# An FNet, adaLN and SwiGLU block: the sequence DFT folded once more, with only every 32nd line corrected

## The chip, the cores and the metric

The kernel runs on one core of one Trainium2 chip. The metric is the device time of one execution in microseconds (us). Each kernel is executed several times; the median and the lowest and highest time are given. A profile of one further execution shows each engine: TensorE (PE, matrix products), VectorE (DVE), ScalarE (ACT), GpSimd (POOL) and SyncE (SP), and the 16 DMA engines. ScalarE, SyncE and GpSimd start the transfers.

## The reference, cut to what matters

S = 2048 rows, D = 512, F = 1792, one batch, all in f32.

```python
def _A_ref(x, dft_seq_re, dft_seq_im, dft_hid_re, dft_hid_im):
    a = jnp.einsum("bsd,ed->bse", x, dft_hid_re)
    b = jnp.einsum("bsd,ed->bse", x, dft_hid_im)
    return jnp.einsum("ts,bse->bte", dft_seq_re, a) - jnp.einsum("ts,bse->bte", dft_seq_im, b)

def _B_ref(x, w1, w3, w2):
    gate = jnp.einsum("bsd,df->bsf", x, w1)
    up = jnp.einsum("bsd,df->bsf", x, w3)
    return jnp.einsum("bsf,fd->bsd", _silu(gate) * up, w2)

mod = (_silu(c) @ w_mod).reshape(c.shape[0], 6, 1, -1)
sa, ca, ga, sb, cb, gb = (mod[:, 0], ..., mod[:, 5])
h = _layernorm(x, axis=-1) * (1 + ca) + sa
x = x + ga * _A_ref(h, ...)          # real part of a DFT over rows and columns
h = _layernorm(x, axis=-1) * (1 + cb) + sb
x = x + gb * _B_ref(h, ...)          # SwiGLU
```

`dft_seq_re` and `dft_seq_im` are 2048x2048 inputs, cos and sin of -2 pi t s / S; a kernel may use their symmetry only if it also verifies it on the chip.

## The kernel before, in words

`folded` is the main path. Every f32 product that must be exact is split into a high and a low part (type fp32r) and done in three passes, high by high, high by low, low by high (`PASSES`). `copy` and `minus` make the parts: ScalarE copies the high part (L87), VectorE subtracts for the low part (L90). Names that end in `h` and `l` are such parts. `minus`, `plus` and `times` (L90, L93, L96) are the VectorE helpers; nearly all its work carries their lines.

**Stage 1, hidden DFT.** Eight blocks k pair 128 rows with the 128 rows mirrored to them. For each: `load_x`, `norm_stats` (L456), scale, `turn_rows` (PE transposes, L492), `modulate_rows`, sums and differences of mirrored rows (`mirror_sums`, tile `hs`), their parts `hh`, `hl`, then `hid_product` (L566, 24 matmuls of 128x256), `hid_difference` (L583) and `hid_mirror` (L605, L614: the DFT of the mirrored rows alone, which serves the correction). The results are `us`, `ul` (sums' high and low part) and `uh`. The order is set by `arrange`, a list planner: each task has a rank, the tasks it needs, and an engine with an assumed time. Before the stage's data are there, `keep_warm` issues matmuls on zeros.

**Stage 2, sequence DFT.** 16 steps of two `seq_unit` each (real and imaginary, m = 0, 1), each 24 matmuls of 128x512 (L757), summed in all 8 PSUM banks. The symmetry halves the rows that must be multiplied: high parts `bh` of the matrix lines are used, plus the tiles `l` and `d`, the differences of the lines from what exact symmetry would give, so any deviation is corrected in full. `load_seq` reads the whole matrix for that (tiles `re`, `im`): 64 direct loads on SP and 64 gathers of mirrored lines on POOL (`load_mirror`, L170). `prepare_seq` makes `bh`, `l`, `d` on VectorE; ScalarE sums their squares (`square`, L188). `residual` (L813) adds the gated result to x.

**Stage 3, SwiGLU.** The second norm, `ln2`, is feature-major (L825 and on): sums over partitions through VectorE's 32x32 transposes. It goes in pieces on the queue `background`, which `advance` and `drain` empty beside the matmuls. Up-products of the first two column groups g = 0, 1 for the first half of the tokens (pair 0) are plain (`up_block`); the others are items (g, pair) and use `factor`, seven products in place of eight (Strassen's form), units a1 to a7 (w1) and b1 to b7 (w3). Down-products are plain (`down_unit`), except in the list `SEVEN` (pair 1, g = 0 to 4), where `seven_unit` does them by seven products. Each y of 512 KB is added to `sums` in HBM by an accumulating DMA on POOL; the last go from SBUF to the output. Near the end `judge` reduces the squares to a flag `bad`; where it is set, `general`, a kernel without the symmetry, runs.

VectorE and ScalarE work in program order, so an instruction that waits holds all that are behind it on that engine. SP and POOL issue their transfers in order too.

Of the kernel before, what the change touches and what calls it, by code (L numbers as in the profile page):

```python
# [15 lines left out]
P = 128  # L16
# [14 lines left out]
AHEAD = 3  # L31
# [11 lines left out]
def folded(nc, pools, c, cp, wmr, wmc, x, xt, ctr, cti, wdr, wdi, w1, w3, w2, out):  # L43

    consts, small, big, psum, dram, tc = pools


# [15 lines left out]
    def bank(i):  # L70
        count[0] += 1
        return psum.tile([P, N], F32, name=f"bank{i}_{count[0]}", tag=f"bank{i}")
# [36 lines left out]

    background = deque()  # L110
    credit = [0.0, 0.0]
# [5 lines left out]
    def advance(dve, act=9.0, queue=background):  # L117

        for n, us in enumerate((dve, act)):
            credit[n] = min(credit[n] + us, max(us, 1.0))  # L120
        while queue and len(free) >= queue[0][0] + kept():
            _, *cost, fn = queue[0]
            if any(us > 0 and credit[n] <= 0 for n, us in enumerate(cost)):
                return
            queue.popleft()
            if fn is None:
                return
            for n, us in enumerate(cost):
                credit[n] -= us
            fn()  # L130

    def drain(ready, queue=background):
# [6 lines left out]
    loads = deque()  # L139

    def kept():
        return 2 if loads else 0


    def where(k):
        return k % (NK // 2), 1 - k // (NK // 2)

    mirror = consts.tile([P, NT, 2, NK // 2], I32, name="mirror")  # L150
    flips = consts.tile([P, 2, NT, 2, NK // 2], I32, name="flips")
    nc.gpsimd.iota(
        mirror, [[S, NT], [2, 2], [-2 * P, NK // 2]], base=S - 1, channel_multiplier=-2
    )
    nc.gpsimd.iota(
        flips[:, 0], [[0, NT], [0, 2], [0, NK // 2]], base=0, channel_multiplier=1
    )
    nc.gpsimd.memset(flips[:, 1], 0)
    nc.gpsimd.memset(flips[0:2, 1, :, 1], 1 - 2 * P)
    nc.gpsimd.memset(flips[0:1, 1, :, 1], -1)  # L160
    nc.gpsimd.memset(flips[0:1, 1, :, 1, 0:1], -1 - S // 2)
    nc.vector.tensor_scalar(flips[:, 0], flips[:, 0], 1, None, op0=OP.bitwise_and)
    for n in range(2):
        plus(mirror, mirror, flips[:, n])

    def load_mirror(dst, src, k, t=None):
        i, par = where(k)
        rows = src.rearrange("i p q n -> (i p q) n" if t is None else "t i p q n -> (t i p q) n")
        at = mirror[:, t or 0, 1 - par, i : i + 1]
        nc.gpsimd.indirect_dma_start(  # L170
            dst, None, rows, bass.IndirectOffsetOnAxis(ap=at, axis=0)
        )

    KINDS = ("re", "im", "wr", "wi")
    chk = consts.tile([P, 2, 4, 32], F32, name="chk")
    nc.gpsimd.memset(chk, 0.0)
    used = {}

    def square(kind, m, src, junk):
# [12 lines left out]
        return n  # L194

# [6 lines left out]
    def load_x(k, other=nc.sync):  # L202
        if k >= NK // 2:
            nc.gpsimd.tensor_copy(held, wd[0][0:1, 1, 0:1].bitcast(F32))


        i, par = where(k)
        xz[k] = take(F32, "x")
        nc.sync.dma_start(xz[k][:, 0, :], x[i][par::2])
        if par:  # L210
            other.dma_start(xz[k][:, 1, :], x[NK - 1 - i][1::2])
        else:
            load_mirror(xz[k][:, 1, :], x, k)
# [7 lines left out]

# [10 lines left out]

    nc.sync.dma_start(cc, cp)
    load_x(0, nc.scalar)
# [9 lines left out]
    for k in range(2, 4):  # L244
        load_x(k)

# [30 lines left out]

    def keep_warm(count, width=N):

# [6 lines left out]
    nc.scalar.activation(sc, cc, AF.Silu)  # L286
    nc.scalar.activation(held, eps[0:1, 0:1], AF.Sqrt)
    mod1 = consts.tile([P, 2, ND], F32, name="mod1")
    ga = consts.tile([P, ND], F32, name="ga")
    ga2 = consts.tile([P, ND], F32, name="ga2")  # L290
# [5 lines left out]

# [21 lines left out]

# [25 lines left out]
    sc_row = []  # L344

    def mod_row():
        sc_row.append(take(F32, "scr"))
        nc.sync.dma_start(sc_row[0][:, 0, :], c.broadcast_to([P, D]))
        nc.scalar.activation(sc_row[0][:, 0, :], sc_row[0][:, 0, :], AF.Silu)

    def mod_columns(v, dst):
        w = {}

        def fetch(i):
            w[i] = take(F32, "wmc")
            nc.sync.dma_start(w[i], wmc[v, i])

        def scale(i):
            times(w[i], w[i], sc_row[0][:, 0, :].unsqueeze(1).to_broadcast([P, 2, N]))

        def total(i):
            r1 = small.tile([P, 32], F32, name=f"r1_{v}_{i}", tag="r1")
            nc.vector.tensor_reduce(
                out=r1,
                in_=flat(w[i]).rearrange("p (a b) -> p a b", b=32),
                axis=AX.X,
                op=OP.add,
            )
            nc.vector.tensor_reduce(
                out=dst[:, 2 * i : 2 * i + 2],  # L370
                in_=r1.rearrange("p (a b) -> p a b", b=16),
                axis=AX.X,
                op=OP.add,
            )
            give(w[i])

        def end():
            if dst is cb1:
                nc.vector.tensor_scalar(cb1, cb1, 1.0, None, op0=OP.add)
            if dst is ga:  # L380
                nc.vector.tensor_scalar(ga2, ga, -2.0, None, op0=OP.mult)
            if dst is gb:
                give(sc_row[0])
            done.add(("mod", v))

        for i in range(2):
            step(background, 1, lambda i=i: fetch(i))
        background.extend([PAUSE] * 2)
        for i in range(2):
            step(background, 0, lambda i=i: scale(i), 1.2)  # L390
            step(background, 0, lambda i=i: total(i), 1.3)
        step(background, 0, end, 0.1)


# [10 lines left out]

# [28 lines left out]

# [10 lines left out]

# [18 lines left out]

# [14 lines left out]

    turned, hm, hs, h1 = {}, {}, {}, {}  # L480
    hh, hl = {}, {}

    def sides(t):

# [2161 lines left out]
```

## Time and profile before

| | |
|---|---|
| median of 3 runs | 691.25 us (690.86 to 692.67) |
| span of the profiled execution | 688.6 us |
| TensorE / VectorE busy | 672.4 us (98%) / 586.2 us (85%) |
| ScalarE / GpSimd busy | 452.3 us (66%) / 133.6 us (19%) |
| stage 2 on the chain of waits | 86.19 to 260.5 us |
| moved by DMA | 116.8 MB |

The times in the profile count from the start of its span; the 2.65 us between the span and the median are start and end of the program outside it. A row of the groups reads: line, engine, operation, output and input by the program's names, shapes, count, then busy us, mean ns of one, and idle time of the engine just before, with what ended it. The windows give busy us and instruction counts of each engine for a stretch of time, then the granted TensorE clock, the mean busy share of the DMA engines and GB/s. Matmul durations in the groups (about 390 ns) overlap; their pace is read from the chain.

### The profile page before, as it was taken

The page shows a single profiled execution, that of the slowest core. Times are in us where ns is not written, and L with a number is a line of the kernel's source. Part 1 is how long each engine was busy: PE and PEld are TensorE (multiplying, and loading weights), DVE is VectorE, ACT ScalarE, POOL GpSimd, SP SyncE. Part 2 cuts the span into 40 slices and gives each one's busy share as a digit, 9 for nine tenths or more (in the row PEclk, how much of TensorE's full clock was granted, in tenths as well). Part 3 has the DMA queues.
Part 4 walks back from the last instruction along what each step waited for, and adds up shares of the span by engine and source line. Part 5 has one row for each costly group of instructions (what it writes and reads, how often), then busy time and mean ns, then how long its engine had stood idle before and what let it go on. Part 6 is the DMA issues. An engine that isn't in the chain of part 4 may idle for free.

```text
span 688.6 us, 9030 instructions
## 1 busy us (share of the span) xinstructions
PE 672.4 (98%) x3120; PEld 557.3 (81%) x3120; DVE 586.2 (85%) x944; ACT 452.3 (66%) x753; POOL 133.6 (19%) x156
## 2 busy tenths in 40 slices
PE   7899999999999999999999999999999999999995
PEld 5798888888888888888788888887887888888784
DVE  5999779997999977989997989787998979888464
ACT  6998965455443665663577767867687887877520
POOL 1320273543435000100101101011011112121100
PEclk9999999999999999999999999999999999999999
DMA  8730299797688431263757666466958998999803
GB/s 265 225 123 1 62 363 352 256 304 239 195 285 289 153 148 31 50 135 122 132 135 135 149 153 123 93 116 134 283 89 186 173 203 168 177 218 172 191 31 127
DMA packets 40837, 116.80 MB, mean 170 GB/s; under 512 B 5200, under 2 KB 5456, under 8 KB 40784
## 3 DMA queue, kind: packets, MB, share of 16 engines
q0 software_dynamic: 14512, 50.86, 36.8%
q1 hardware_dynamic: 25840, 63.98, 28.1%
q10 hardware_dynamic: 432, 1.31, 0.6%
q8 instruction: 26, 0.43, 0.3%
q14 instruction: 27, 0.22, 0.1%
HBM read 76.81 MB, written 41.42 MB: 172 GB/s over the span
## 4 chain that ended last, share of the span: by engine, by line
PE 84%; DVE 9%; ACT 3%; DMA 2%; issue 1%; SPq 1%; DVEq 0%; ACTq 0%
PE bank L100 54%; PE bank L757 26%; PE bank L566 2%; PE bank L605 1%; DMA w<-in_wdr 1%; DMA w<-in_wdi 1%; SPq L231 1%; DVE xr L813 1%; PE bank L583 1%; DMA x<-in_x 1%; DVE v L96 1%; DVE hl L90 0%; DVE ul L90 0%; DVE x L93 0%; ACT hm L508 0%
## 5 line engine op out<-in xcount | busy, mean ns | idle before, releaser
L100 PE MATMUL bank<-hf,w2h 128*128 128x512 f32 (+1 forms) x352 | 108.3, 389 | 0.0
L87 ACT ACTIVATE hf<-v 128x512 fp32r<-128x512 f32 x71 | 44.4, 631 | 66.9 <-DVE v L96 56.4
L342 ACT ACTIVATE y<-bank,gb 128x512 f32<-128x512 f32 x118 | 76.6, 683 | 3.9 <-PE bank L100 3.6
L100 PEld LDWEIGHTS bank<-hf,w2h 128*128 128x128 f32 x352 | 65.6, 188 | 15.3 <-ACT y L342 1.4
L1168 POOL DMA_DIRECT2D sum<-y x28 | 24.0, 857 | 240.7 <-ACT y L342 124.5
L100 PE MATMUL bank<-hf,w2l 128*128 128x512 f32 (+1 forms) x176 | 68.1, 387 | 0.0
L90 DVE TENSOR_TENSOR hf<-v,hf 128x512 fp32r<-128x512 f32 x71 | 48.7, 686 | 10.4 <-ACT hf L87 10.3
L1360 POOL DMA_DIRECT2D sum<-y x35 | 29.8, 852 | 128.3 <-ACT y L342 113.7
L87 ACT ACTIVATE x<-bank 128x512 f32<-128x512 f32 x72 | 41.9, 592 | 13.1 <-PE bank L100 12.3
L170 POOL DMA_INDIRECT re<-in_ctr,mirror x32 | 37.0, 1157 | 66.5 <-ACT im L188 40.1
L757 PE MATMUL bank<-bh,us 128*128 128x512 f32 x128 | 49.9, 390 | 0.0
L757 PE MATMUL bank<-bh,ul 128*128 128x512 f32 x128 | 49.8, 389 | 0.0
L757 PE MATMUL bank<-d,us 128*128 128x512 f32 x128 | 49.8, 389 | 0.0
L757 PE MATMUL bank<-d,uh 128*128 128x512 f32 x128 | 49.8, 389 | 0.0
L757 PE MATMUL bank<-l,us 128*128 128x512 f32 x128 | 49.8, 389 | 0.0
L757 PE MATMUL bank<-l,uh 128*128 128x512 f32 x128 | 49.8, 389 | 0.0
L170 POOL DMA_INDIRECT im<-in_cti,mirror x32 | 33.3, 1042 | 31.6 <-PE bank L757 10.0
L100 PEld LDWEIGHTS bank<-hf,w2l 128*128 128x128 f32 x176 | 33.1, 188 | 6.7
L93 DVE TENSOR_TENSOR v<-bank,x 128x512 f32<-128x512 f32 x36 | 24.7, 686 | 15.8 <-PE bank L100 14.9
L1252 ACT ACTIVATE v<-v 128x512 f32<-128x512 f32 x36 | 22.7, 629 | 22.9 <-DVE v L93 22.6
L93 DVE TENSOR_TENSOR x<-bank,x 128x512 f32<-128x512 f32 x36 | 24.7, 685 | 14.8 <-PE bank L100 11.9
L188 ACT ACTIVATE im<-l 128x512 f32<-128x512 f32 x16 | 10.1, 632 | 32.3 <-DVE d L93 15.4
(263 smaller groups left out, 1922.0 us busy)
## 6 DMA issues: line engine op xcount, KB each, us to landing
sum<-y POOLq DMA_DIRECT2D x63, 512.0 KB, 5.6
w<-in_w SPq DMA_DIRECT2D x42, 512.0 KB, 4.8
re<-in_ctr SPq DMA_DIRECT2D x32, 256.0 KB, 5.2
im<-in_cti SPq DMA_DIRECT2D x32, 256.0 KB, 5.7
wmc<-in_wmc SPq DMA_DIRECT2D x8, 512.0 KB, 6.9
sum<-xr SPq DMA_DIRECT2D x8, 512.0 KB, 5.4
x<-in_x SPq DMA_DIRECT2D x11, 256.0 KB, 4.6
xr<-in_xt SPq DMA_DIRECT2D x8, 256.0 KB, 7.6
```

The source lines that it names most:

```text
L87: nc.scalar.activation(dst, src, AF.Copy, scale=scale)
L90: nc.vector.tensor_tensor(out=dst, in0=a, in1=b, op=OP.subtract)
L93: nc.vector.tensor_tensor(out=dst, in0=a, in1=b, op=OP.add)
L100: nc.tensor.matmul(acc, lhs[a], rhs[b], start=first and n == 0, stop=last and n == len(PASSES) - 1, skip_group_check=more,)
L170: nc.gpsimd.indirect_dma_start(dst, None, rows, bass.IndirectOffsetOnAxis(ap=at, axis=0))
L188: nc.scalar.activation(to, src.bitcast(F32), AF.Square, accum_out=chk[:, kind, KINDS.index(m), n : n + 1],)
L342: nc.scalar.activation(dst, src, AF.Identity, scale=by)
L566: nc.tensor.matmul(halves(hb[k])[:, m, :], sides((hh, hl)[a][k])[:, dt, m, :], wu[dt][:, b, m, :], start=False, stop=dt % 2 == 1 and n == ...
L757: nc.tensor.matmul(acc[what, e], lhs, rhs, start=begin and i == 0, stop=(end or (turn and what == "x")) and i == len(terms) - 1, skip_grou ...
L1168: nc.gpsimd.dma_start(sums[t, d // 2], y, accum_op=OP.add)
L1252: behind(k != 0 or q == 0, lambda: nc.scalar.activation(v, src, AF.Silu))
L1360: nc.gpsimd.dma_start(sums[t, which], y, accum_op=OP.add)
```

## The change

Parts named here are new unless a line of before is given.

1. *Sequence DFT, folded once more.* `hid_mirror`, `uh`, `prepare_seq` and `seq_unit` go. The output rows split in even and odd (o) and in mirrored halves; `seq_piece` multiplies only 512 of the 2048 output rows, as four blocks b of 128, by `mh`, `ml` (parts of the matrix, loaded directly by `load_m`). The two banks of a block, m = 0 and 1, are read after the odd part and after all (`read_odd`, `read_all`), and sums and differences of the two (`read_other`, `join`) give the four groups of rows, which `add_rows` adds to x.
2. *Correction.* Only every 32nd line and column is corrected. `stage_lines` copies these columns in HBM to `lines` (16 transfers on SP) and `load_lines` reads them; `line_columns`, `turn_lines`, `line_rows`, `line_products`, `row_products`, `line_pairs`, `line_shares` form small products whose result enters the banks in `seq_lines`. Coefficients per partition (`signs`, `whole`, some 65 VectorE instructions on one column) are made at the very start.
3. *Differences counted.* All other entries are compared for equality: `check_steps` loads the matrix in stage 3 (tiles `cx`, `cz` direct, `cy`, `cv` by gathers) and counts unequal ones on VectorE. They go on the queue `checks`; `PAUSE` entries put about three units between a load and its comparison. What is left over is drained at `J`, ahead of `judge` in the last item, which now also requires a count of 0.
4. *Second norm token-major.* `ln2_stats`, `ln2_scale`, then `turn_block` transposes to feature-major (PE); `keep_sums` stores x to `sums`. These are `arrange` tasks, as are 11 units of the first item.
5. *SwiGLU.* All 14 items use `factor`; `SEVEN` is empty, so all down-products are plain. `mod_columns` becomes `mod_column`.

The core of the diff:

```diff
-    def hid_mirror(k, high):
-    def prepare_seq(n, m):
-    def seq_unit(n, m, between=None):
-    def ln2(t):
...
+    def seq_piece(b, o, m):
+        for a in range(NG4):
+            k = NG4 * o + a
+            for n, (p, q) in enumerate(PASSES):
+                nc.tensor.matmul(acc(b, m), (mh, ml)[p][b, o][:, m, cols(a)],
+                    (us, ul)[q][k][:, m, :], ...)
...
+    def read_odd(b, m):
+        nc.vector.scalar_tensor_tensor(
+            pq[b][m][:, 1, :], acc(b, m), -2.0, gar[0][:, 0, :], op0=OP.mult, op1=OP.mult)
+    def read_all(b, m):
+        times(pq[b][m][:, 0, :], acc(b, m), gar[0][:, 0, :])
...
+        if n == 0:
+            plus(flat(u), flat(p), flat(q))
+        elif n == 2:
+            minus(flat(p), flat(p), flat(q))
...
+        def differs(n, a, b, by, at=None):
+            nc.vector.scalar_tensor_tensor(
+                out, a, by, b, op0=OP.mult, op1=OP.not_equal, accum_out=at)
...
+        step(checks, 5, lambda: (load("x"), load("y")))
+        checks.extend([PAUSE] * 3)
+        step(checks, 3, lambda: main(0), 0.7)
+        step(checks, 0, lambda: main(1), 1.2)
...
+            if what == "J":
+                drain(lambda: not checks, checks)
+                judge()
...
-    SEVEN = [(g, 1) for g in range(NG - 2)]
+    SEVEN = []
```

How this stands in the engines' order, at three places. On VectorE, the start, up to the first norm statistics (`BN_STATS`); before:

```order
L162 TENSOR_SCALAR flips<-flips 128x32
L93 ISA mirror<-mirror,flips 128x64 x2
L248 MEMSET eps 128x1
L275 MEMSET tmp_142 128x512
L456 BN_STATS st_0_166<-x_87 128x6
```

and changed, the last eleven rows up to the same place (47 rows of the same kind, `mirror` and `signs`, stand ahead of them):

```order
L398 TENSOR_TENSOR signs<-signs 128x1
L395 TENSOR_SCALAR signs<-signs 128x1 x3
L455 MEMSET signs 128x2
L456 MEMSET signs 32x1
L457 MEMSET signs 32x1
L459 CAST mask<-whole 128x1
L395 TENSOR_SCALAR signs<-signs 128x1
L461 TENSOR_SCALAR mask<-mask 128x1
L462 TENSOR_SCALAR signs<-signs 128x1
L398 TENSOR_TENSOR signs<-signs 128x1
L604 BN_STATS st_0_284<-x_108 128x6
```

The coefficients stand ahead of all work on x. On TensorE, the change from stage 2 to SwiGLU (`L100` before, `L93` changed, is SwiGLU's product); before:

```order
L757 MATMUL bank_269_1846<-d_2428,us_1057 128x512
L757 MATMUL bank_269_1846<-d_2428,uh_1061 128x512
L757 MATMUL bank_271_1848<-d_2428,us_1057 128x512
L757 MATMUL bank_271_1848<-d_2428,uh_1061 128x512
L100 MATMUL bank_351_2574<-h2h_2449,w1h_2487 128x512
```

and changed:

```order
L1079 MATMUL banks<-us_1281,ml_1869 128x512
L1109 MATMUL banks<-ya_274,er_909 128x512
L1109 MATMUL banks<-z_268 128x512
L1109 MATMUL banks<-ya_274,sel_334 128x512
L1109 MATMUL banks<-ya_274,er_909 128x512
L1109 MATMUL banks<-ya_274,sel_334 128x512
L93 MATMUL banks<-h2h_1756,w1h_1593 128x512
```

SwiGLU's first product now follows `seq_lines` of the last block. On POOL, a stretch of SwiGLU; before:

```order
L1168 DMA sum_0_2266<-y_3328 128x1024
L1168 DMA sum_1_2268<-y_3364 128x1024
L1168 DMA sum_0_2635<-y_3412 128x1024
L1168 DMA sum_1_2637<-y_3465 128x1024
L1168 DMA sum_0_2266<-y_3595 128x1024
```

and changed:

```order
L217 DMA cv_4559<-in_cti,mirror 128x512 x2
L1599 DMA sum_0_2008<-y_4583 128x1024
L217 DMA cy_4607<-in_ctr,mirror 128x512 x2
L1599 DMA sum_1_2108<-y_4618 128x1024
L1599 DMA sum_0_2166<-y_4664 128x1024
L217 DMA cv_4719<-in_ctr,mirror 128x512 x2
```

The gathers of the comparison stand between the accumulations of y.

More of the change, by code (lines that the diff above doesn't have):

```diff
@@ L29 @@
 SLOTS = 50
-AHEAD = 3
+LOG = None
 LEAD = 3
@@ L70, in bank @@
     def bank(i):
-        count[0] += 1
-        return psum.tile([P, N], F32, name=f"bank{i}_{count[0]}", tag=f"bank{i}")
+        return banks[:, i, :]
     def flat(t):
@@ L157, in folded @@
     )
[L158 to L169, printed above, removed]
+    nc.gpsimd.memset(rows_of[0:1, 0, 0, 0:1], S // 2)
@@ L1025, in judge @@
             in_=chk.rearrange("p a b n -> p (a b) n"),
+            axis=AX.X,
+            op=OP.add,
+        )
+        nc.vector.tensor_reduce(
+            out=sq[:, 0, 8:9],
+            in_=cnt.rearrange("p a b c d -> p (a b c d)"),
             axis=AX.X,
```

1636 lines of the change are left out of this document (1036 added, 600 removed).

## The prediction

> **What bounds the kernel now.** I read the page first: busy times, the slices, the chain by engine and line.
>
> ```profile
> span 688.6 us, 9030 instructions
> ...
> PE 672.4 (98%) x3120; PEld 557.3 (81%) x3120; DVE 586.2 (85%) x944; ACT 452.3 (66%) x753; POOL 133.6 (19%) x156
> ...
> PE   7899999999999999999999999999999999999995
> ...
> DVE  5999779997999977989997989787998979888464
> ...
> PE 84%; DVE 9%; ACT 3%; DMA 2%; issue 1%; SPq 1%; DVEq 0%; ACTq 0%
> ```
>
> TensorE has work 98% of the time and the chain runs through it; VectorE, at 85%, is the next limit. The executions shown have a median of 691.25 us, 2.65 above this span, which I add at the end. Their scatter, 690.86 to 692.67, makes 0.3% (2 us) about what a measurement can tell from no change.
>
> Then the busy time by stage (hidden DFT, sequence DFT, SwiGLU, tail), and the chain in order of time for the pace.
>
> ```profile
> core 0: us, PE busy (x) PEld busy (x) DVE busy (x) ACT busy (x) POOL busy (x), PEclk, DMA share, GB/s
> 0.00:86.20 86.20, 77.98 (x505) 68.02 (x506) 72.32 (x151) 73.71 (x149) 16.41 (x32) 1.00 0.46 135
> 86.20:260.50 174.30, 174.30 (x769) 144.22 (x769) 157.71 (x220) 93.12 (x178) 63.15 (x61) 1.00 0.74 255
> 260.50:681.70 421.20, 420.10 (x1849) 345.07 (x1847) 355.75 (x574) 285.45 (x427) 54.02 (x64) 1.00 0.67 143
> 681.70:688.60 6.90, 0.00 (x0) 0.00 (x0) 0.46 (x1) 0.00 (x0) 0.00 (x0) 0.78 0.25 86
> ...
> 86.19 174.32 PE bank L757 x768
> ...
> 524.15 103.67 PE bank L100 x456
> ```
>
> The sequence stage is 768 matmuls without a hole: 174.32/768 = 0.227 us for a 128x512 one, the same in SwiGLU (103.67/456 = 0.227). So a matmul taken out here is worth 0.227 us, but only until VectorE, busy 157.7 of those 174.3 us, becomes the bound.
>
> **TensorE's part of the change.** Smaller matmuls are priced by their pieces of the chain:
>
> ```profile
> 29.87 0.95 PE bank L492 x8
> ...
> 31.99 1.44 PE bank L566 x12
> ```
>
> A 128x128 f32 transpose takes 0.119 us (0.95/8), a 128x256 product 0.120 (1.44/12). Removed: 776 matmuls of the sequence sum and 84 of the mirrored hidden rows, 860 x 0.227 = 195.2 us. Added: 192 `seq_piece` and 49 `seq_lines` (54.7); 160 transposes, 128 of them for the token-major norm (19.0); 64 f32 products of 128x128 in `line_rows` (7.6 by the transpose's row; 14.5 if they take as long as a 128x512 one; I take 7.6, same shape and type); 72 small products for the lines (8.6); 44 more warming matmuls, at most 5; SwiGLU 1848 for 1842 (1.4). Together 96 to 103, so TensorE loses 92 to 99 us of work. Its factored down-products for pair 1 go (+30 matmuls), and the up-products of the first pair gain the factor (-24).
>
> **VectorE's part.** This now decides the time before SwiGLU, because its work there falls much less. Rows by shape:
>
> ```profile
> L456 DVE BATCH_NORM_STATS2 st<-x 128x6 f32<-128x512 f32 x16 | 10.9, 680 | 3.3 <-DMA x<-in_x 3.3
> ...
> L90 DVE TENSOR_TENSOR hs<-hm 128x512 f32<-128x512 f32 x8 | 5.5, 691 | 0.0
> ...
> L813 DVE SCALAR_TENSOR_TENSOR xr<-bank,ga,xr 128x512 f32<-128x512 f32 x16 | 11.1, 745 | 4.8 <-PE bank L757 4.7
> ...
> L90 DVE TENSOR_TENSOR w1l<-w,w1h 128x1024 fp32r<-128x1024 f32 x14 | 17.1, 1219 | 0.3 <-ACT w1h L87 0.3
> ...
> L477 DVE TENSOR_SCALAR x<-x,rs 128x512 f32<-128x512 f32 x11 | 5.7, 545 | 0.3
> ...
> L846 DVE COPY q<-r 32x16 f32<-32x16 f32 x32 | 5.5, 170 | 0.4
> ...
> L90 DVE TENSOR_TENSOR w1s<-w1s,w 128x256 f32<-128x256 f32 x12 | 5.1, 425 | 0.4
> ```
>
> In the changed program's VectorE order I count what stands up to the bank read (`read_all` of block 2) that frees the first SwiGLU bank: 35 of 128x1024 at 1.22 (42.7), 53 of 128x512 at 0.687 (36.4), 37 scalar_tensor_tensor at 0.745 (27.6), 24 norm statistics at 0.68 (16.3), 20 of 128x256 at 0.42 (8.4), 15 at 0.545 (8.2), 118 tiny ones at 0.16 (18.9; the row says 0.17 with neighbours overlapped) and 7.9 of others: 166.4. The same count for before, to the end of its hidden stage, gives 80.0, where VectorE was busy 72.3 (adjacent instructions overlap), a factor of 0.904. So 150.4 us busy. To this comes idle time:
>
> - As before in the hidden stage: 86.2 - 72.3 = 13.9, less the 3.3 for the first x, now covered by some 65 tiny instructions on `signs` and 13 for mirrors. They stand ahead of the first statistics, most waiting for the one in front: 12.9 us, so these start near 14 instead of 5.8. Their work is counted above; 10.6 of idle stays.
> - The lines. SP issues 16 staging copies and their loads ahead of later row blocks:
>
> ```profile
> 12.04 0.59 SPq L209
> ...
> x<-in_x SPq DMA_DIRECT2D x11, 256.0 KB, 4.6
> ...
> re<-in_ctr SPq DMA_DIRECT2D x32, 256.0 KB, 5.2
> ```
>
> An issue takes 0.59. About 50 issues (30 us) from the first wait, then a store and a gather of about 5 us each, place the lines near 45 to 50 us, and x of block 4 near 55 to 60. VectorE reaches these places some 3 and 5.5 us earlier: 8.5. Bounds 0 (the counts of VectorE lag further) and 17 (twice).
> - The last line product: transposes, squares, `gs` and `gm` follow one another through three engines, then lead to the first `seq_lines`. Ten to fifteen steps of 0.5 to 0.7 us with other work between: 9.5, bounds 0 and 15.
> - Sequence units and their bank reads alternate at the end: a unit of 24 to 28 matmuls takes 5.4 to 6.4 us, and VectorE lacks other work for about 7 in all; bounds 3 and 15.
>
> 150.4 + 10.6 + 8.5 + 9.5 + 7 = 186. The first SwiGLU matmul, at 260.5 before, so comes at 186. From there to unit b2 of the second item VectorE has 56.6 us of work (same rows; blocks 2 and 3 still pass through sums and norm beside SwiGLU's bank reads), TensorE 174 matmuls, 39.5 us. I take VectorE's 56.6 unshortened, as the two alternate: b2 at 243, and 1674 matmuls of 0.227 (380) are left: 623.
>
> **What SwiGLU takes over.** The matrix, 33.5 MB in 64 direct loads and 64 gathers, is read here instead of in the sequence stage, and compared: 48 instructions of 128x32x31 (1.22, the row of 1024 elements; at 0.745/0.687 of it 1.32), 16 of 128x16x31 (0.745), 64 of 128x2x16 (0.16): 81 us of VectorE. It drops the feature-major second norm from there. What is left for those 1674 matmuls is 342.9 by the rows, 320 by the overlap of this stage, 84% of 380; before it is 355.75 of 421.2, 84%. So VectorE isn't SwiGLU's limit on average.
>
> For DMA: before, the sequence stage spent 0.74 x 174.3 = 129 us of DMA time on 44 MB, so 33.5 MB cost 97; SwiGLU's 0.67 x 421.2 = 282 become 379 of some 440, a share of 0.86, without the 15 accumulations into `sum` that go (63 to 48). On POOL the gathers now stand in one line with the accumulations, each waiting for its `y`:
>
> ```profile
> q0 software_dynamic: 14512, 50.86, 36.8%
> ...
> L170 POOL DMA_INDIRECT re<-in_ctr,mirror x32 | 37.0, 1157 | 66.5 <-ACT im L188 40.1
> L1168 POOL DMA_DIRECT2D sum<-y x28 | 24.0, 857 | 240.7 <-ACT y L342 124.5
> ...
> sum<-y POOLq DMA_DIRECT2D x63, 512.0 KB, 5.6
> ```
>
> Both together are 64 x 1.16 + 48 x 0.86 = 115 us of POOL, which has room. A load starts three units (4 us or more) ahead of its comparison, and a gather lands in 5 or 6 us: some comparisons will wait. VectorE takes work in order, so the bank reads behind such a comparison wait too, and TensorE waits when the next unit wants that bank. Before, SwiGLU lost 421.2 - 1842 x 0.227 = 3 us; the bounds are 3 and 64 x 0.3 = 20, and I take 8, since each unit leaves VectorE 16% of slack. The comparisons left over and the flag come near the end, about 7.5 us of VectorE against 6.7 us of matmuls: 4 with load waits (0 to 8). The tail stays 6.9.
>
> Sum: 623 + 8 + 4 + 6.9 = 642, and with 2.65 **645 us**, 6.7% less than 691.25. ScalarE doesn't enter: 684 instructions become 571, and 285 of 421 us were busy.
>
> **The clock.** Before, TensorE was full; in the changed first 186 us it has about 100 us of work and waits often. The one stretch of before that looks so is its start:
>
> ```profile
> 0.00:5.00 5.00, 2.40 (x3) 1.18 (x4) 1.06 (x5) 2.36 (x3) 2.98 (x16) 1.00 0.52 111
> 5.00:10.00 5.00, 3.28 (x12) 1.64 (x11) 3.63 (x9) 3.40 (x8) 0.00 (x0) 1.00 1.02 403
> ```
>
> The granted clock reads 1.00 there, with the engine busy 5.7 of 10 us, so I charge nothing. The Trainium skill (TensorE: Matmul & The Clock Gate, "What's actually happening") speaks against that: after an idle window of about 3.4 us the clock is halved, until about 3.4 us of work have passed. By that figure eight such waits would cost at most 8 x 1.7 = 14 us, an estimate from the page, and the sum would be 659; the rows cited have no hole of that length after work, so this trace can't decide.
>
> **Rivals.**
> 1. *TensorE stays the bound* (8%): VectorE's idle time vanishes and the first item is hidden. Then the span falls by 92 to 99: 590 to 597, with 2.65 and the same holes, 592 to 600. For it: only TensorE is near full now. Against it: 166 us of VectorE work ahead of a stage whose matmuls need 100.
> 2. *The clock falls in the waits* (10%): if waits of the first 186 us make half of its 100 us of matmuls run at half pace, that is 50 us more TensorE work, of which VectorE's surplus hides about 30: 665.
> 3. *The comparisons stall SwiGLU, and the kernel gets slower* (5%): gathers queued on POOL behind an accumulation that waits for `y`. It decides from 46 us on, 46/64 = 0.72 us past the slack at every gather; at 1 us each, 64 - 8 = 56 more: 701. For it: DMA share rising from 0.67 to 0.86. Against it: the sequence stage ran 64 gathers at 0.74 without a hole.
> 4. *The flag is raised and the general branch runs* (1%): off the 32nd lines the mirrored entries of the matrices that the reference builds are equal to the bit, so the counts are 0; otherwise the whole transform would run again, far over 1000 us.
>
> **How the numbers follow.** My forecast, VectorE as bound to 186 us and SwiGLU at TensorE's pace, has 76%. Its low end takes half the idle (-18), half of VectorE's excess in the first item and a half (56.6 - 39.5 = 17, so -9) and stalls as before (-5): 612. Its high end doubles the estimated idle of lines and units (+22) and takes 20 + 8 for the stalls and the flag (+16), less what can't come together: 680, which holds rival 2. Outside are rival 1, and rivals 3 and 4 above. Slower: 5 + 1%; no change 2%, the edge of rival 3; faster 92%.
>
> **What would show it.** The first `L93` matmul near 186 us, VectorE near 85% ahead of it and TensorE near 55%; first statistics at 14; SwiGLU's matmuls at 0.227, its DMA share near 0.8; a few us of TensorE waiting in it for banks read behind `cj`. I am wrong if TensorE is full from 60 us on (rival 1), if the granted clock is under 0.9 ahead of SwiGLU (2), or if waits for `cy` and `cv` sum to over 40 us (3).

## The result, and the profile after

The changed kernel takes **767.97 us** (median of 4 runs, 760.14 to 770.85) against 691.1 us: a ratio of 1.109, 95% interval 1.103 to 1.115. It is 77 us slower, where 645 us and 46 us faster was predicted. Of the kernels below, `e3_loads_only` and `f_s15x4` each had one execution far longer than the others (1546 and 1020 us); their medians are those of the other three.

The page of the changed kernel: span and busy times, the slices of TensorE, VectorE and the granted clock, and the chain by engine.

```profile
span 765.3 us, 8815 instructions
...
PE 634.7 (83%) x2966; PEld 517.7 (68%) x2966; DVE 531.6 (69%) x1080; ACT 368.1 (48%) x578; POOL 167.8 (22%) x169
...
PE   2956798899887689699997999798999999945961
...
DVE  8849774538999556559776786895767878643771
...
PEclk8979899899978699899999999999999999978976
...
issue 43%; PE 17%; DMA 12%; POOL 12%; DVE 9%; SPq 3%; ACT 3%; POOLq 0%; DVEq 0%; ACTq 0%
```

TensorE's busy time fell by 38 us (672.4 to 634.7) and VectorE's by 55, and yet the span grew: no engine is full on average any more. DMA and POOL (its gathers) now hold 24% of the chain. "issue" in it is time that the profile doesn't resolve (one such piece runs from 189 to 283 us), so for the stages I go by the windows (the bounds are the first `L93` matmul at 220.8, and the end of the matmuls at 750).

```profile
core 0: us, PE busy (x) PEld busy (x) DVE busy (x) ACT busy (x) POOL busy (x), PEclk, DMA share, GB/s
0.00:93.00 93.00, 60.67 (x410) 54.61 (x410) 71.25 (x209) 48.17 (x99) 34.60 (x47) 0.85 0.44 136
93.00:186.00 93.00, 82.12 (x480) 68.37 (x480) 53.83 (x105) 37.78 (x67) 8.17 (x9) 0.94 0.42 125
186.00:220.80 34.80, 32.12 (x144) 23.97 (x144) 33.16 (x48) 18.06 (x22) 0.00 (x0) 0.90 0.29 94
220.80:277.00 56.20, 42.17 (x173) 33.05 (x174) 42.37 (x72) 31.00 (x44) 0.00 (x0) 0.79 0.28 102
277.00:660.00 383.00, 352.81 (x1509) 286.12 (x1508) 276.58 (x527) 212.66 (x318) 110.71 (x99) 0.97 0.83 193
660.00:750.00 90.00, 64.81 (x255) 51.59 (x253) 53.91 (x124) 20.41 (x32) 14.33 (x14) 0.85 0.50 125
750.00:766.00 16.00, 0.00 (x0) 0.00 (x0) 0.48 (x1) 0.00 (x0) 0.00 (x0) 0.58 0.20 58
```

Laid beside the prediction's sum (the 174th `L93` matmul is that of unit b2 of the second item, the place the prediction counted to):

| stretch | predicted | measured | |
|---|---|---|---|
| to the first SwiGLU matmul | 186 | 220.8 | +35 |
| to b2 of the second item | 57 | 76.8 | +20 |
| the other 1674 matmuls, stalls, flag | 392 | 452.3 | +60 |
| tail | 6.9 | 15.4 | +8.5 |
| span | 642 | 765.3 | +123 |

Half of the miss lies in SwiGLU proper. VectorE's waits there (us in total, times, longest), and then TensorE's:

```profile
DVE cj L1419 <- DMA cv<-in_ctr,mirror: 22.8, 5, 7.2
...
DVE cj L1419 <- DMA cx<-in_ctr: 13.4, 2, 10.7
DVE cj L1419 <- DMA cz<-in_cti: 12.4, 2, 11.0
DVE cj L1419 <- DMA cv<-in_cti,mirror: 9.9, 3, 4.3
...
DVE cj L1419 <- DMA cx<-in_cti: 7.3, 1, 7.3
DVE cj L1419 <- DMA cy<-in_cti,mirror: 6.7, 4, 5.0
...
DVE cj L1419 <- DMA cy<-in_ctr,mirror: 5.2, 4, 2.2
```
```profile
PE banks L93 <- DVE hf L83: 22.9, 7, 6.1
PE banks L93 <- DVE x L86: 12.7, 4, 10.4
PE banks L93 <- DVE xr L1590: 7.7, 1, 7.7
PE banks L93 <- ACT hf L80: 6.6, 1, 6.6
```

The comparisons (`cj`, L1419) wait 80 us for their parts of the matrix (these rows, and 2.6 for the other `cz`), and TensorE then waits for VectorE's work behind them. One such case in order of time, on POOL, VectorE and TensorE (start, duration, and in brackets the idle time before and what ended it):

```profile
403.44 0.89 POOL L1599 DMA_DIRECT2D sum<-y  x1 [5.80 <-ACT y L526]
404.64 1.07 POOL L217 DMA_INDIRECT cv<-in_ctr,mirror  x1 [0.31 <-DVE cj L1419]
406.02 1.93 POOL L217 DMA_INDIRECT cv<-in_ctr,mirror  x1 [0.30 <-issue]
```
```profile
408.20 0.68 DVE L89 TENSOR_TENSOR v<-v,banks 128x512 f32<-128x512 f32 x1
414.88 1.19 DVE L1419 SCALAR_TENSOR_TENSOR cj<-cz,cv 128x992 f32<-128x992 f32 x1 [6.00 <-DMA cv<-in_ctr,mirror]
```
```profile
418.06 0.79 PE L93 MATMUL banks<-hf,w2h 128*128 128x512 f32 x1 [5.22 <-DVE hf L83]
418.66 0.63 PE L93 MATMUL banks<-hf,w2l 128*128 128x512 f32 x1
419.08 1.05 PE L93 MATMUL banks<-hf,w2h 128*128 128x512 f32 x2
...
421.58 0.39 PE L93 MATMUL banks<-th,w1sh 128*128 128x512 f32 x1
421.81 0.40 PE L93 MATMUL banks<-tl,w1sh 128*128 128x512 f32 x1
```

A tile is loaded by two gathers. They are issued at 404.6 and 406.0, behind an accumulation that had waited 5.8 us for its `y`; VectorE arrives at 408.9, 4.2 us behind the first and 2.9 behind the second, and the data land at 414.9. VectorE then makes up its backlog, TensorE stands still for 5.2 us, and its next matmuls follow at 0.42 us apart instead of 0.23 for 3.4 us.

### The profile page after: what moved, and what is told of

Its sections match the earlier page's. It is cut to its first block, busy times and chain, and to the rows that moved or that the text cites. A ratio compares the mean times of both kernels' runs of the same rounds, so it can differ in the third digit from the quotient of the medians.

```text
span 765.3 us, 8815 instructions
## 1 busy us (share of the span) xinstructions
PE 634.7 (83%) x2966; PEld 517.7 (68%) x2966; DVE 531.6 (69%) x1080; ACT 368.1 (48%) x578; POOL 167.8 (22%) x169
## 4 chain that ended last, share of the span: by engine, by line
issue 43%; PE 17%; DMA 12%; POOL 12%; DVE 9%; SPq 3%; ACT 3%; POOLq 0%; DVEq 0%; ACTq 0%
PE banks L93 8%; POOL cy L217 4%; POOL sum L1599 4%; PE banks L1079 4%; POOL cv L217 3%; DMA cy<-in_ctr,mirror 3%; DMA cv<-in_ctr,mirror 2%; DMA cx<-in_ctr 2%; PE banks L733 1%; PE banks L1109 1%; DVE cj L1419 1%; DMA wmc<-in_wmc 1%; DMA cz<-in_ctr 1%; SPq L1043 1%; DMA wmr<-in_wmr 1%
## 5 line engine op out<-in xcount | busy, mean ns | idle before, releaser
L93 PE MATMUL banks<-hf,w2h 128*128 128x512 f32 (+1 forms) x452 | 148.5, 408 | 38.1 <-DVE hf L83 22.9
L93 PEld LDWEIGHTS banks<-hf,w2h 128*128 128x128 f32 x452 | 88.9, 198 | 61.8 <-DVE hf L83 27.1
L93 PE MATMUL banks<-hf,w2l 128*128 128x512 f32 (+1 forms) x226 | 91.2, 403 | 0.0
L526 ACT ACTIVATE y<-banks,gb 128x512 f32<-128x512 f32 x96 | 65.6, 683 | 33.9 <-PE banks L93 31.7
L1683 ACT ACTIVATE v<-v 128x512 f32<-128x512 f32 x42 | 26.5, 630 | 64.0 <-DVE v L86 61.3
L80 ACT ACTIVATE x<-banks 128x512 f32<-128x512 f32 x84 | 48.9, 590 | 16.7 <-PE banks L93 14.5
L93 PEld LDWEIGHTS banks<-hf,w2l 128*128 128x128 f32 x226 | 44.7, 198 | 9.1
L1419 DVE SCALAR_TENSOR_TENSOR cj<-cz,cv 128x992 f32<-128x992 f32 x16 | 19.0, 1189 | 32.8 <-DMA cv<-in_ctr,mirror 22.8
L93 PE MATMUL banks<-th,w1sh 128*128 128x512 f32 x84 | 34.4, 410 | 4.2 <-ACT x L80 3.5
L93 PE MATMUL banks<-tl,w1sh 128*128 128x512 f32 x84 | 34.0, 405 | 0.0
L93 PE MATMUL banks<-th,w1sl 128*128 128x512 f32 x84 | 33.9, 403 | 0.0
L93 PE MATMUL banks<-th,w3sh 128*128 128x512 f32 x84 | 33.1, 394 | 0.0
L93 PE MATMUL banks<-tl,w3sh 128*128 128x512 f32 x84 | 32.9, 392 | 0.0
L93 PE MATMUL banks<-th,w3sl 128*128 128x512 f32 x84 | 32.8, 390 | 0.0
L1419 DVE SCALAR_TENSOR_TENSOR cj<-cx,cz 128x992 f32<-128x992 f32 x16 | 19.0, 1185 | 15.0 <-DMA cz<-in_cti 12.4
```

The costliest lines, as they stand in the source:

```text
L80: nc.scalar.activation(dst, src, AF.Copy, scale=scale)
L93: nc.tensor.matmul(acc, lhs[a], rhs[b], start=first and n == 0, stop=last and n == len(PASSES) - 1, skip_group_check=more,)
L526: nc.scalar.activation(dst, src, AF.Identity, scale=by)
L1419: nc.vector.scalar_tensor_tensor(out, a, by, b, op0=OP.mult, op1=OP.not_equal, accum_out=at)
L1683: behind(k != 0 or q == 0, lambda: nc.scalar.activation(v, src, AF.Silu))
```

## Experiments

The ratios are to the kernel before in the same set of runs, with 95% intervals; kernels of different sets are compared by their ratios. A ratio can differ from the quotient of the two medians by some 0.002, and differences in us are of medians. The comparisons are left out in `e1_no_checks`, in all kernels whose label begins with `b_`, and in `c_floor`, `d_x7` and `f_two`; `e2_compares_only` compares one pair of tiles again and again, `e3_loads_only` loads and compares nothing. Theory A is that late comparison data stall VectorE and through it TensorE; its rivals, that the VectorE work of the comparisons is too much, or that their loads alone slow everything else.

**The comparisons taken apart.** `e1_no_checks`:

```diff
-    for k in range(NK):
-        for m in range(2):
-            check_steps(k, m)
```


> Left out: the loads and comparisons of check_steps (nothing is counted). Theory A (VectorE, in order, waits for a comparison's load, and TensorE for VectorE): the 1674 matmuls behind unit b2 of the second item took 452 us against 392 forecast; without comparisons they take 385 to 400, the kernel about 708 (700 to 720). Theory B (the loads' share of the DMA engines slows weights and accumulations) and theory C (the 81 us of comparing work itself) expect the same of this kernel. Theory D (TensorE's gaps and its halved clock come from the token-major norm and the banks, not from the comparisons): over 740.

706.38 us, 1.023 (1.020 to 1.026): 61.6 us less than with them (59 by the ratios).

`e2_compares_only` loads one pair of tiles once and runs the comparisons on it (only `x` and `y`, 16 times in the same places):

```diff
-        step(checks, 5, lambda: (load("x"), load("y")))
+        if len(check_sets) == 1:
+            step(checks, 5, lambda: [load(x) for x in "xy"])
...
-        for m in range(2):
-            check_steps(k, m)
+    for n in range(16):
+        check_steps(0, 0)
```


> All 64 large and 64 small comparisons stay on VectorE, but on two tiles loaded once, so 62 of the 64 tile loads are gone (the third and fourth large comparison of a set repeat the second). A: the waits go, within 10 us of the kernel without comparisons, about 712. C: the work is what costs, over 740.

710.28 us, 1.028 (1.026 to 1.031): the VectorE work costs 4 us.

`e3_loads_only` keeps every load in its place, without an instruction that reads it:

```diff
-        step(checks, 3, lambda: main(0), 0.7)
-        step(checks, 0, lambda: main(1), 1.2)
-        step(checks, 0, lambda: (small_one("x"), small_one("y"), leave_all("y")), 0.4)
+        step(checks, 0, lambda: leave_all("y"))
...
```


> All loads of check_steps stay, nothing is compared. A: about 712, since nobody waits for the loads. B: contention alone costs, over 740, with longer landings of w and y than in the kernel without comparisons.

716.12 us, 1.036 (1.032 to 1.039): the loads alone cost 9.7 us. In its trace this isn't a slower pace throughout: TensorE's waits behind unit b2 of the second item sum to 14.8 us, against 4.9 in `e1_no_checks`, and the longest follows weights (`w`) that came late to VectorE, at a DMA share of 1.05 from 500 to 520 us:

```profile
525.61 0.42 DVE L86 TENSOR_TENSOR w3s<-w 128x256 f32<-128x256 f32 x1 [6.06 <-DMA w<-in_w]
...
530.17 0.79 PE L93 MATMUL banks<-th,w3h 128*128 128x512 f32 x1 [6.47 <-DVE x L86]
```

Work and loads make 13.6 of 61.6 us; the other 48 appear only where a comparison waits for its load. What the waits took away shows in the SwiGLU windows of `e1_no_checks`:

```profile
220.90:277.00 56.10, 41.93 (x172) 32.99 (x173) 42.16 (x71) 30.71 (x44) 0.00 (x0) 0.79 0.28 102
277.00:640.00 363.00, 359.19 (x1573) 294.55 (x1572) 227.16 (x334) 225.65 (x331) 41.76 (x49) 1.00 0.64 131
```

From 277 us on TensorE is 99% busy at a clock of 1.00, and its 1674 matmuls take 389.4 us: the prediction's pace, which was 380 and some stalls. With the comparisons they take 452.3, 62.9 more. TensorE's waits account for 47.6 of these (52.5 against 4.9); most of the rest is the same matmuls at a slower pace, 399.6 us busy against 384.8.

`e4_lead` issues each load one section of comparisons earlier:

```diff
-        step(checks, 2, lambda: load("v"))
-        checks.extend([PAUSE] * 3)
+        more = next_set(k, m)
+        if more:
+            step(checks, 8, lambda: (more[0]("x"), more[0]("y")))
+        checks.extend([PAUSE] * 2)
...
```


> Every load is issued one section earlier, 4 pauses ahead of its comparison with other comparisons between, instead of 3 directly ahead. A: VectorE's waits for cx, cy, cz, cv fall from 79 us to under 40, the kernel to 725 to 745. B or C: no change, 760 to 775.

729.03 us, 1.055 (1.051 to 1.059): 39 us of the 61.6 are won back by nothing but earlier issues. Waits for comparison data fall from 80 to 33 us; the longest kind left is `cz` (10.0 us). Theory A stands. It was tried once more from the other side below (`c_p1`).

**The rest, without comparisons.** `e1_no_checks` has some 95 us less of TensorE work than the kernel before, by the prediction's count, and is still slower. By stages, from the two profiles: the first SwiGLU matmul comes 39.6 us sooner (220.9 for 260.5); the 174 matmuls after it take 78.5 us for 39.5 (174 x 0.227), the 1674 then 7.7 more (389.4 for 381.7), the tail 6.8 more. Each of the next kernels takes one suspected wait away from it.

`b_tail` issues the last transfers from two engines:

```diff
+    out_queue = [nc.sync, nc.scalar]
...
-                nc.sync.dma_start(out
+                out_queue.reverse()
+                out_queue[0].dma_start(out
```


> The kernel without comparisons (706 us), with the 32 final transfers issued in turn by SP and ScalarE instead of by SP alone. Theory: SP's issue, 32 x 0.6 = 19 us, sets the tail (15.4 us from the last matmul to the end, 6.9 before), so the tail falls to about 8 and the kernel to about 699. Rival: the landing of the transfers sets it; no change, 705 to 708.

701.83 us, 1.014 (1.011 to 1.017), 0.009 less. The time from the last matmul to the end falls from 13.5 to 9.9 us; about 8 was expected. In the changed kernel SyncE issues the last 32 transfers one after the other, 0.6 us each, until 7 us before the span's end; the kernel before had 9 of them in 8 us:

```profile
739.24 19.09 SPq L1563 DMA_DIRECT2D out<-xr  x32
```

`b_rows` moves three small copies that wait for a late line row from ScalarE to GpSimd:

```diff
-            copy(zz[:65, 1, :], src[:65])
-            copy(zw, z512)
-            copy(wz[:, :, 0, :], w512)
+            nc.gpsimd.tensor_copy(zz[:65, 1, :], src[:65])
+            nc.gpsimd.tensor_copy(zw, z512)
+            nc.gpsimd.tensor_copy(wz[:, :, 0, :], w512)
```


> The kernel without comparisons, with the copies of the late line row (z from br) on GpSimd instead of ScalarE, where they held everything behind them from 39 to 47 us and VectorE with it for 9.3. Theory: in-order ScalarE is the cause and the delay is passed on to SwiGLU's start; 697 to 701. Rival: it is given back at later waits (x of block 4 lands late too, wmc lands at 132); 704 to 708.

697.98 us, 1.009 (1.006 to 1.011), 0.015 less. In the changed kernel ScalarE stands 8 us before the first of them, and what VectorE needs from ScalarE stands behind it:

```profile
46.91 0.63 ACT L80 ACTIVATE z<-br 65x512 fp32r<-65x512 f32 x1 [7.98 <-POOL held L256]
```

Without that the first SwiGLU matmul comes at 216.9 instead of 220.9. A step of that size is near what two traces can differ by: `b_tail`, which changes nothing ahead of that matmul, has it at 223.2.

`b_mod` ranks the columns of the modulation, which read late loads of 512 KB, later:

```diff
-   f"modv{v}.{i}.{q}", 8 * PACE - 20 + 10 * v,
+   f"modv{v}.{i}.{q}", 8 * PACE - 20 + 25 * v,
```


> The kernel without comparisons, with the column sums of the modulation (mod_column for v = 1 to 3) ranked 15, 30 and 45 later, so that VectorE doesn't wait for wmc (10.4 us of waits at 116 to 140) ahead of the bank reads of the hidden stage. Theory: the wait is passed on, gain 5 to 10: 696 to 701. Rival: TensorE's sequence units are held by other things there (mh from m, ScalarE's squares): 704 to 708.

698.33 us, 1.010 (1.006 to 1.014), 0.013 less; the first SwiGLU matmul at 215.1. The four waits behind this, and the other of VectorE's two longest ahead of SwiGLU in the changed kernel (the second is the one that `b_rows` removes: it has no such wait, and `b_mod` has 1.0 us left of the first):

```profile
DVE wmc L535 <- DMA wmc<-in_wmc: 10.4, 4, 5.1
DVE hs L86 <- issue: 9.3, 1, 9.3
```

`b_signs` puts the some 65 tiny instructions on `signs` on GpSimd:

```diff
-        nc.vector.tensor_scalar(col(dst), col(src), a, b, op0=op0, op1=op1)
+        nc.gpsimd.tensor_scalar(col(dst), col(src), a, b, op0=op0, op1=op1)
...
```


> The kernel without comparisons, with the coefficients (signs, some 55 tiny instructions) made on GpSimd, so that the first norm statistics come near 6 instead of 14.4 us. Theory: VectorE's work ahead of SwiGLU sets its start, 8 to 10 us are gained: 696 to 698. Rival: the lines, staged by SP at 26 to 41 us, hold the stage anyway: 704 to 708, and the coefficients on GpSimd come too late for the gathers: slower.

706.31 us, 1.020 (1.016 to 1.023): no gain that can be told. One instruction on `mask` had stayed at the head of VectorE, waited 12.7 us for GpSimd there, and the first statistics came at 18.1 us. As built it decides nothing, so `b_signs2` moves that instruction to the flag:

```diff
-    nc.vector.tensor_scalar(mask, mask, 0.0, None, op0=OP.not_equal)
...
     def judge():
+        nc.vector.tensor_scalar(mask, mask, 0.0, None, op0=OP.not_equal)
```


> As the first trial with the coefficients on GpSimd, but the one VectorE instruction on them (mask) stands at the flag instead of ahead of the first norm statistics, where VectorE waited 12.7 us for it. Theory: first statistics near 6 instead of 14.4, gain 5 to 10 against 706: 696 to 701. Rival: the stage is held by what follows (the late lines, wmc, the sequence units): 703 to 708.

704.92 us, 1.020 (1.018 to 1.022). The first statistics come at 8.0 us, but those of the next late block at 53.1, as before: ScalarE's wait for the line row stands in between, and VectorE's wait for `hs` behind it grows from 9.3 to 15.1 us. The gain at the head meets a later wait there and is given back, as far as these runs can tell.

`c_floor` puts `b_tail`, `b_rows`, `b_mod` and `b_signs2` together.

> Without comparisons, with four changes together: line row on GpSimd (measured alone: -8.4), later column sums (-8.0), final transfers by two engines (-4.5), coefficients on GpSimd. If the gains add: 676 to 686, below the kernel before. If they hide one another (one wait taken, the next one ends last): 688 to 695.

686.02 us, 0.991 (0.988 to 0.994). The first SwiGLU matmul is at 206.8, 14 us sooner, and the whole is 0.032 less, where the three that gained alone make 0.037. So the change without its comparisons, and with these four repairs, gains 0.9%, not the 46 us that were predicted. What still holds 207 against 186 was tried in two more.

`d_x7` lets the lines' loads follow seven row blocks on SyncE instead of preceding them:

```diff
-    load_task("lines", 3.5, ["w3"], load_lines, 6, 6.0)
+    load_task("lines", 3.5, ["w3", "x7.q"], load_lines, 6, 6.0)
```


> The version with all four changes and without comparisons, whose first SwiGLU matmul came at 206.8 us and which took 686.02, with one thing more: the tasks that load the lines stand on SyncE behind the load of the seventh row block instead of ahead of it. In that version the statistics of block 4 came at 52.8 us, because its rows wait on SyncE behind the lines. Theory: the late rows hold the whole first stage; then those statistics come near 45, the first SwiGLU matmul near 199 and the run takes 676 to 682. Rival: the stage from 128 us to the first SwiGLU matmul is set by what follows the lines (TensorE was busy 54.2 of 57 us there), and lines that come later make it later: the first SwiGLU matmul at 206 to 212 and 685 to 691. Comparisons are left out, so it is no whole computation.

685.96 us, 0.992 (0.990 to 0.995): nothing, and my theory of late rows falls. The later of VectorE's two waits for `x` goes, and a longer wait for the broadcast line takes its place, first in `c_floor`, then in `d_x7`:

```profile
47.05 0.75 DVE L932 SCALAR_TENSOR_TENSOR ef<-br,signs,dl 128x512 f32<-128x512 f32 x1 [3.80 <-POOL br L316]
```
```profile
53.07 0.75 DVE L932 SCALAR_TENSOR_TENSOR ef<-br,signs,dl 128x512 f32<-128x512 f32 x1 [10.43 <-POOL br L316]
```

`f_two` leaves out 64 of the 192 matmuls of the sequence sum (those with `ul`):

```diff
             for n, (p, q) in enumerate(PASSES):
+                if q:
+                    continue
```


> The same version of 686.02 us without the 64 matmuls of the sequence sum that take the low half of the positions' weights: 64 x 0.227 = 14.5 us of TensorE ahead of SwiGLU, nothing else moved (the low halves are still made). Theory (TensorE holds the stretch from 128 us to the first SwiGLU matmul, which the prediction added up by VectorE alone): that matmul comes 10 to 14.5 us sooner, at 192 to 197, and the run takes 672 to 678. Rival (VectorE or the chain of lines holds it): at 203 to 207, and 682 to 687. Comparisons and this third of the sequence sum are left out.

679.98 us, 0.982 (0.977 to 0.986), 0.009 (0.004 to 0.014) less than `c_floor`; the first SwiGLU matmul at 200.2. 14.5 us of TensorE's work were taken away and 6.6 came off: between the two theories. I read this as TensorE holding about half of the stretch; what holds the rest wasn't tried. In `c_floor`, ahead of that matmul, TensorE was busy 54.2 of 57 us:

```profile
150.00:207.00 57.00, 54.20 (x237) 38.75 (x236) 46.46 (x68) 24.06 (x28) 1.89 (x2) 0.94 0.25 79
```

**The whole computation again.** `c_s15` takes the four repairs and the earlier loads; the last two sets load earlier still, and the flag stands five units later:

```diff
-        step(checks, 2, lambda: load("v"))
-        checks.extend([PAUSE] * 3)
+        more = next_set(k, m)
+        if more:
+            step(checks, 9, lambda: (more[0]("x"), more[0]("y")))
+        checks.extend([PAUSE] * 2)
...
-            body = "a6 y a5 y b1 a7 y a3 y b2 a4 y b6 y b5 y b7 J y b4 y b3 " + "y " * 9
+            body = "a6 y a5 y b1 a7 y a3 y b2 a4 y b6 y b5 y b7 y b4 y b3 " + "y " * 5 + "J " + "y " * 5
```


> The whole computation with every comparison: the four changes together, loads issued one section ahead (4 pauses) as measured at 729 before, those of the last two sets as early as the tiles allow, and the flag five units later. If the waits for loads at the end are gone: about 15 above the kernel without comparisons, 692 to 700; if SP's and GpSimd's order still holds the loads back, 705 or more.

700.43 us, 1.012 (1.009 to 1.014): 68 us better than the change as it was, and 1.2% slower than the kernel before. `c_p1` is the same with one pause between the steps instead of two, and without the special order of the last two sets, so that each load leads by less:

```diff
-        checks.extend([PAUSE] * 2)
+        checks.extend([PAUSE] * 1)
...
```


> As the last, but 2 pauses per load instead of 4, so that all comparisons end ahead of the flag. Theory (lead decides): more waiting for loads than with 4 pauses, 700 to 712. Rival (the drained rest at the end was the cost): 690 to 698.

747.31 us, 1.079 (1.076 to 1.082). Same loads, same work, 47 us more, in the direction expected but far beyond the 712 that was its bound. The direct load of `cx` from `in_ctr` shows it: in `c_p1`, behind the first set, four times it is issued 3.7 to 4.0 us ahead of VectorE, lands after 8.0 to 9.1 and keeps VectorE waiting for 4.3 to 5.4; where VectorE waits for `cx` in `c_s15`, it leads by 8.2 to 8.4, lands after 8.6 to 10.0, and the wait is 0.4 to 1.6. With the sums of the waits of `cj` for DMA, and the price against the same kernel without comparisons:

| kernel | waits for data | price |
|---|---|---|
| changed | 80 | 61.6 over `e1_no_checks` |
| `c_p1` | 76 | 61.3 over `c_floor` |
| `e4_lead` | 33 | 22.7 over `e1_no_checks` |
| `c_s15` | 32 | 14.4 over `c_floor` |

`f_s15x7` and `f_s15x4` add the later lines of `d_x7` (after the seventh, and after the fourth block) to `c_s15`:

```diff
-    load_task("lines", 3.5, ["w3"], load_lines, 6, 6.0)
+    load_task("lines", 3.5, ["w3", "x7.q"], load_lines, 6, 6.0)
```


> The whole computation: the version that took 700.43 (four changes, loads one section ahead), with the lines' loads behind the seventh row block on SyncE. Theory (late rows hold the first stage): 690 to 697, level with the kernel before or a little under. Rival (what follows the lines holds it): 699 to 706.

707.15 us, 1.022 (1.018 to 1.026).

> The whole computation as in the version of 700.43, with the lines' loads behind the fourth row block alone, so that the lines lose less time. Theory (late rows hold the first stage): between the version of 700.43 and the one with seven blocks ahead, 693 to 699. Rival (what follows the lines holds it): 699 to 703, less late than with seven blocks.

705.85 us, 1.020 (1.012 to 1.027), outside the ranges of both theories. Neither helps; with seven blocks ahead it is slower by 0.010, VectorE's wait for the broadcast line grows from 6.5 to 11.0 us, and the first SwiGLU matmul moves from 206.7 to 212.8. In `d_x7` the same edit moved that matmul by 1 us only, so how far the stage waits for the lines stays open. No version with the whole computation beat the kernel before.

## Why the prediction was wrong, point by point

- **The stalls of SwiGLU (8 us taken, 3 to 20 as bounds).** This is the largest miss. The mechanism was named, as rival 3, with 5%, and even there it stopped at 701, gathers alone counted. The prediction gave a load a lead of 4 us or more and a landing of 5 or 6, and priced the shortfall at 0.3 us a gather. Neither the landing nor the lead held. In the kernel before, gathers landed in 6.4 and 5.4 us, with the stage at a DMA share of 0.74; at the 0.83 of 277 to 660 us in the changed one some took far longer (median us from issue to landing, last number; first before, then changed):

```profile
re<-in_ctr,mirror POOLq DMA_INDIRECT x32, 6.4
im<-in_cti,mirror POOLq DMA_INDIRECT x32, 5.4
```
```profile
cy<-in_ctr,mirror POOLq DMA_INDIRECT x14, 7.9
cv<-in_ctr,mirror POOLq DMA_INDIRECT x14, 9.5
```

  The lead fell short too. Of the 80 us of waits, 48 belong to eight loads whose issue (of a gather pair, the second) began less than 4 us ahead of VectorE, 0.7 to 3.7. In the case shown the gathers stood behind an accumulation that waited for its `y`, as rival 3 has it. Nor were gathers alone late: `cx` and `cz`, direct loads from SyncE, account for 36 of the 80 us. The two longest waits, 11.0 and 10.7 us, are of this kind. SyncE stood there in front of the reloads of `sum` (`xr`), which wait for the accumulations (40.9 us in four waits), and the comparison's loads stood behind:

```profile
660.29 7.72 SPq L1553 DMA_DIRECT2D xr<-sum  x2
668.11 1.26 SPq L185 DMA_DIRECT2D cz<-in_cti  x2
671.17 19.62 SPq L1553 DMA_DIRECT2D xr<-sum  x2
...
691.36 1.72 SPq L185 DMA_DIRECT2D cx<-in_ctr  x2
```

  VectorE was at these two comparisons by 668.8 and 693.5, and could start them at 679.8 and 704.2; the DMA share between the issue and that start was 0.85 and 0.96. The point from which the rival decides (46 us) was passed by 15, with 61.6. The 16% of slack on VectorE covered the comparing work (4 us in `e2_compares_only`) but not the waits, since slack of the mean doesn't help the matmul that waits now.
- **186 us to the first SwiGLU matmul.** The first statistics at 14 were right (14.4), and nearly right was the count of VectorE's work: 158.2 us busy up to 220.8 (its three windows) against 150.4. Idle is 62.6 us, not 36. Two waits were missing: ScalarE held 8 us by the line row, and the `wmc` loads (10.4), both shown by their removal (0.015 and 0.013 of the time). With all four repairs the matmul still comes at 206.8; the 21 us from there to 186 are explained only in part. The term "sequence units and their bank reads alternate: 7" was mis-sized: the prediction's sum runs along VectorE alone, with TensorE near 55%, but TensorE was busy 88% of 93 to 186 us and 92% after. The stage is two bounds one after the other, VectorE and the lines first, then a block of sequence sums that needs the hidden stage's results; by `f_two`, about half of what its matmuls cost is on the path, 6.6 of 14.5 us.
- **57 us for the first item.** Here too two engines take turns. To 260 us VectorE is busy 36.4 of 39.2 us, and from there to b2 TensorE is busy 33.8 of 37.6:

```profile
220.80:260.00 39.20, 26.36 (x107) 19.88 (x107) 36.44 (x61) 20.35 (x28) 0.00 (x0) 0.80 0.18 65
260.00:277.00 17.00, 15.81 (x67) 13.17 (x68) 5.93 (x11) 10.65 (x16) 0.00 (x0) 0.77 0.51 186
277.00:297.60 20.60, 17.98 (x84) 14.27 (x83) 8.92 (x13) 12.80 (x20) 5.04 (x5) 1.00 0.73 170
```

  The prediction took the larger of two totals, 56.6 and 39.5; the sum of both phases is 76.8. It stays at 78 in `c_floor` and `f_two`, so it isn't an echo of what comes before. No run took VectorE's part of it away.
- **The clock.** Rival 2's sign came: a granted clock of 0.85 in the first 93 us, 0.90 over the 220.8 ahead of SwiGLU and 0.79 just behind, from a forecast of no charge. In five-us windows:

```profile
225.00:230.00 5.00, 3.77 (x11) 2.64 (x12) 5.00 (x9) 1.81 (x3) 0.00 (x0) 0.69 0.00 0
230.00:235.00 5.00, 3.24 (x8) 2.06 (x7) 4.91 (x5) 1.60 (x3) 0.00 (x0) 0.50 0.00 0
```

  After a 5.2 us hole the matmuls at 418 came 0.42 us apart, until 421.5. By the rule that the prediction weighed (the Trainium skill, TensorE: Matmul & The Clock Gate, "What's actually happening"), the trace agrees: half the clock after an idle window, for about 3.4 us. What the clock alone cost wasn't tried: it comes with the waits, and 8 matmuls at 0.2 us more make 1.6 us, an estimate, at each such hole. Behind b2 the matmuls were busy 14.8 us longer in the changed kernel than in `e1_no_checks`, about the most that it can have cost there.
- **Tail 6.9.** It is 15.4, with 32 transfers leaving one queue where there were 9. The prediction had the 0.59 us of an issue in a row and didn't use it here. `b_tail` gets 0.009 back.
- **Right:** 0.227 us for a matmul and 392 us for the 1674 (389.4 without comparisons); the forecast that TensorE doesn't stay the bound (rival 1); the general branch not taken; the DMA share of SwiGLU (0.86 forecast; 0.83 from 277 to 660 us, 0.77 from 298 to 750). The 92 to 99 us of work taken from TensorE aren't settled: its busy time fell by 38 only, but a matmul that stands alone counts there with its full 0.39 us, and a cold one with 0.63.
- **What I said would prove me wrong did:** waits for `cy` and `cv` over 40 us (44.6, with `cx` and `cz` 80), and a clock under 0.9 in the first 93 us, though not over the whole stretch.

## What to carry to other kernels

An engine that works in order turns a late load into a wait of everything behind it; price each such load by its landing at the DMA share to come less its lead, not by the mean slack of the engine, and count the lead from when its queue gets to the load's last transfer, not from where the load stands in the program. When TensorE's work is cut and the rest is ready in phases, the time is the sum of phases, each with its own bound, and not the total of the engine that is next in line: write down what each phase waits for before adding. And a gain at the head is worth nothing until the next wait in order is known to move with it (`b_signs2`, `d_x7`).

## What the runs showed of the hardware

Transfers landed later in the stage with the higher DMA share, short of 1: `sum<-y` took 6.5 us (median) at 0.83 and 5.6 in the SwiGLU stage of before, at 0.67; gathers took 6.4 to 9.5 at 0.83 and 5.4 and 6.4 in the kernel before, in a stage at 0.74. Whether the share makes the difference, or what else stands in the queue, wasn't separated. Loads of the comparisons cost 9.7 us even when nothing reads them (`e3_loads_only`). Short waits were enough to bring the granted clock down: from 223.8 to 228 us TensorE stood still for 1.8 and 0.65 us with 1.8 us of matmuls between, after which matmuls came 0.42 us apart; the granted clock was 0.50 from 230 to 235.
